# Zero-tile multiplications on TensorE during the first loads and maxima of an attention and two-layer kernel

## Chip, cores, metric

The kernel runs on one core of a Trainium2 chip. The metric is the device time of one execution in microseconds; lower is better. Engines are named as in the profile: PE is TensorE's matmul, PEld its weight load, DVE is VectorE, ACT ScalarE, POOL GpSimd, SP the engine that issues most DMAs.

## What is computed

Attention with queries that are averaged in pairs, then two feed-forward layers on its output (2304 tokens, width 512, inner width 2048):

```python
# q, k, v: (4, 8, 1152, 64)
q_pool = q.reshape(B, H, S // 2, 2, D).mean(axis=3)
scores = np.matmul(q_pool, k.transpose(0, 1, 3, 2)) / np.sqrt(D)
scores = scores - np.max(scores, axis=-1, keepdims=True)
attn = np.exp(scores)
attn = attn / (np.sum(attn, axis=-1, keepdims=True) + 1e-09)
x = np.matmul(attn, v)            # heads side by side: 2304 x 512
h = x @ moe_w_in
x = (h - np.tanh(h)) @ moe_w_out
r = np.maximum(x @ moe2_w_in, 0.0)
out = (s * (r * r) + b) @ moe2_w_out
```

## The kernel before

Attention goes by pairs of heads, 16 pairs. `prep(n)` prepares pair n: it adds neighbouring queries (L355), transposes queries (`ptq`, L361) and keys (`ptk`, L380) on TensorE, splits them into a rounded part and a rest (`U`, `T`, `ql`, `kl`), sends pieces to other partitions by DMA on SP's queue, and computes the maximum of every query's scores. For that it multiplies 128 queries by 384 keys into a PSUM tile `ptm` (L418 for pair 0, L420 for later pairs, L394 for the queries that are left over, `ptm_r`), and VectorE reduces each tile to one column (L421, L395). The loop runs over the two heads j, over groups s of 128 queries (four) and over key blocks i (three), so a head has twelve such steps. The maxima of a head are reduced once more (L423), transposed (`ptc`, L425) and moved to a row of `U2`, which the second part of each score multiplication (L460) takes in. `scores` computes transposed scores in two multiplications, L459 with 128 rows and L460 with 65, takes the exponential on ScalarE (L461), and `single` multiplies the result by the values (L532).

For pair 0 alone (L416 to L418) the maxima take one head's half of the partitions, so these multiplications have 64 rows; all others named here have 128 or 65 rows. PSUM tiles of `prep` come from a ring of four (`psP`).

While pair 0's maxima are computed, pair 1's queries and keys are loaded. All but the first two key loads are issued on SP's queue, in order. The tile framework keeps one order for each engine, and an engine takes its instructions strictly in that order. Pair 0's steps, pair 1's transposes and the first scores are interleaved in it by a clock of ticks; `tc.high_priority` moves an instruction ahead and `tc.issue_after` holds it behind another.

`rests` are two tiles of 128 x 128 that start as zeros; `prep(n)` writes the left-over queries of pair n into `rests[n % 2]` (L369).

Of the kernel before, what the change touches and what calls it, by code (L numbers as in the profile page):

```python
# [9 lines left out]
F32 = mybir.dt.float32  # L10
F32R = mybir.dt.float32r
# [7 lines left out]
P = 128  # L19
# [28 lines left out]
BATCH = 3  # L48
STORE, PUT = 8, 6
LINE, TOP = 32, 24  # L50

MOE_NS = 445
EVAC_NS = 250
# [2 lines left out]
SOON = 40  # L56
# [3 lines left out]
def f32(ap):  # L60
    return ap.bitcast(F32)
# [3 lines left out]
def attention_moe_moe_kernel(  # L65
# [19 lines left out]
    HB = SQ // 2  # L85
# [17 lines left out]
    mm = nc.tensor.matmul  # L103
    act = nc.scalar.activation
    dve = nc.vector
# [7 lines left out]
    pp = pctx.enter_context(tc.tile_pool(name="prep", bufs=1))  # L113
    fp = sctx.enter_context(tc.tile_pool(name="fin", bufs=1, side="right"))
    swp = sctx.enter_context(tc.tile_pool(name="sweep", bufs=1, side="right"))
    stage = actx.enter_context(tc.tile_pool(name="stage", bufs=1, side="right"))

    ident = cp.tile([P, P], F32, name="ident")
    make_identity(nc, ident)
# [35 lines left out]
    def line(pool, n, name, tag=None):  # L155
        return pool.tile([P, -(-n // LINE) * LINE], F32, tag=tag or name, name=name)[:, :n]

    def later(k, fn):
        queue.append((clock[0] + k, fn))
# [13 lines left out]
    class Weights:  # L173
# [63 lines left out]
        def put(self, which, f, i, cols, x):  # L237
            w = weight(f)
            if self.left > self.act_last:
                dve.tensor_copy(w[:, 2 * i, cols], x)  # L240
            else:
                act(w[:, 2 * i, cols], x, AF.Copy)
            added[0] = self.sub(w[:, 2 * i + 1, cols], x, f32(w[:, 2 * i, cols]))
# [61 lines left out]
    psV = actx.enter_context(tc.tile_pool(name="psV", bufs=1, space=PSUM))  # L305
# [17 lines left out]
    for j in range(2):  # L323
        dve.memset(f32(T2[j][D:D + 1, :]), 1.0)

    rests = [pp.tile([P, P], F32R, name=f"rest{i}") for i in range(2)]
    for rest in rests:
        dve.memset(f32(rest), 0.0)

    ops = {}  # L330

    def load_pair(n):
        b, hp = pairs[n]
        h0 = 2 * hp
        for j in range(2):
            dma(out=qrs[j], in_=q[b, h0 + j].rearrange("(t p r) d -> p t (r d)", p=QP, r=2))
        for j in range(2):
            put = nc.scalar.dma_start if n == 0 else dma
            put(out=kr[:, :, j, :], in_=k[b, h0 + j].rearrange("(p t) d -> p t d", t=NKT))
# [5 lines left out]
    def prep(n):  # L345

        T1, U1, ql = T1s[n % 3], U1s[n % 3], qls[n % 2]
        rest = rests[n % 2]
        kl = T1s[2][0] if n == 0 else kl1
        ops[n] = (T1, U1)  # L350

        for j in range(2):
            eng = dve if n == 0 else pool
            with tc.issue_after(added[0].ins) if n > 1 else ExitStack():
                eng.tensor_add(qrs[0][:, :, j * D:(j + 1) * D], qrs[j][:, :, 0:D], qrs[j][:, :, D:2 * D])  # L355
        yield 4 if n < 2 else 16
        for g in range(2):
            with tc.high_priority(offset=SOON):
                pt = psP.tile([P, KB], F32, tag="pp", name=f"ptq{n}_{g}")
                for i in range(3):  # L360
                    nc.tensor.transpose(  # L361
                        pt[:, i * QP:(i + 1) * QP],
                        qrs[0][:, 3 * g + i],
                        ident[:QP, :QP],
                    )
                act(U1[1][:, g * HB:(g + 1) * HB], pt[:, :HB], AF.Copy)
                h = slice((1 - g) * D, (2 - g) * D)
                q0 = g * (HB - MIX)
                act(rest[h, (1 - g) * MIX:(2 - g) * MIX], pt[h, q0:q0 + MIX], AF.Copy)  # L369
                dve.tensor_sub(  # L370
                    ql[:, g * HB:(g + 1) * HB], pt[:, :HB], f32(U1[1][:, g * HB:(g + 1) * HB])
                )
            yield 2
        for i in range(2):
            dma(out=f32(U1[0][i * D:(i + 1) * D, :]), in_=f32(U1[1][0:D, :]))
        for g in range(NKB):
            with tc.high_priority(offset=SOON):
                pt = psP.tile([P, KB], F32, tag="pp", name=f"ptk{n}_{g}")
                for i in range(3):
                    nc.tensor.transpose(  # L380
                        pt[:, i * P:(i + 1) * P],
                        kr[:, 3 * g + i].rearrange("p h d -> p (h d)"), ident)
                act(T1[1][:, g * KB:(g + 1) * KB], pt, AF.Copy)
                dve.tensor_sub(
                    kl[:, g * KB:(g + 1) * KB], pt, f32(T1[1][:, g * KB:(g + 1) * KB])
                )
            yield 2
        dma(out=f32(T1[0][0:D, :]), in_=f32(T1[1][0:D, :]))
        moved[0] = dma(out=f32(T1[0][D:P, :]), in_=f32(kl[0:D, :]))
        mps = [line(ap, (NQS + 1 - j) * NKB, f"mp{n}_{j}", f"mp{j}").rearrange("p (s i) -> p s i", i=NKB)  # L390
               for j in range(2)]
        for i in range(NKB):
            pt = psP.tile([P, KB], F32, tag="pp", name=f"ptm{n}_r_{i}")
            mm(pt, rest, T1[1][:, i * KB:(i + 1) * KB], start=True, stop=True)  # L394
            dve.reduce_max(mps[0][:, NQS, i:i + 1], pt, axis=AX.X)  # L395
            yield MAXSTEP
        def rest_moves():
            with tc.issue_after(moved[0].ins):
                dma(out=f32(U1[1][0:D, :]), in_=f32(U1[1][D:P, :]))
                dma(out=f32(T1[1][0:D, :]), in_=f32(kl[D:P, :]))  # L400

        if n > 0:
            rest_moves()
        if n + 1 < len(pairs):
            later(LOAD, lambda: load_pair(n + 1))
        yield GAP1 if n == 1 else GAP
        for j in range(2):
            ns = NQS + 1 - j
            mp = mps[j]
            m = line(ap, ns, f"m{n}_{j}", f"m{j}")  # L410
            for s in range(NQS):
                for i in range(NKB):
                    pt = psP.tile([P, KB], F32, tag="pp", name=f"ptm{n}_{j}_{s}_{i}")
                    kk = slice(i * KB, (i + 1) * KB)
                    q0 = s * P + j * MIX
                    if n == 0:  # L416
                        h = slice(j * D, (j + 1) * D)
                        mm(pt, U1[1][h, q0:q0 + P], T1[1][h, kk], start=True, stop=True)  # L418
                    else:
                        mm(pt, U1[j][:, q0:q0 + P], T1[j][:, kk], start=True, stop=True)  # L420
                    newest[0] = dve.reduce_max(mp[:, s, i:i + 1], pt, axis=AX.X)  # L421
                    yield MAXSTEP
            dve.reduce_max(m, mp, axis=AX.X)  # L423
            pt = psP.tile([P, KB], F32, tag="pp", name=f"ptc{n}_{j}")
            nc.tensor.transpose(pt[:ns, :P], m, ident)  # L425
            act(cs[j], pt[:ns, :P], AF.Copy, scale=-1.0)
            maxes.add((n, j))
            if n == 0 and j == 1:
                rest_moves()
            yield 1  # L430
# [235 lines left out]


    load_pair(0)
    moe = deque()
    preps = deque()  # L670
    pend = deque()

    def add_prep(n):
        preps.append([prep(n), clock[0]])
# [346 lines left out]
    for t in range(2):  # L1021
        for i in range(NBLK3):
            for p in range(t * RUN, (t + 1) * RUN):
# [13 lines left out]
                for x, (a, b) in enumerate(PRODUCTS):  # L1037
                    ps = Y if b in ("b21", "t1", "b22") else X
                    fresh_ = b in ("b11", "b21", "t1")
                    for h, (wa, xa) in enumerate(((0, 0), (0, 1), (1, 0))):  # L1040
                        for c in range(2):
                            mm(ps, u[a][:, (2 * wa + c) * P:(2 * wa + c + 1) * P], xs[b][xa][:, c],  # L1042
                               start=(fresh_ and h == 0 and c == 0), stop=(h == 2 and c == 1), skip_group_check=not fresh_)
# [73 lines left out]
```

## Time and profile before

| | us |
|---|---|
| median of 3 runs | 1342.68 |
| the three runs | 1341.97, 1342.68, 1345.07 |
| the profiled execution | 1345.31 |
| its span in the trace | 1343.5 |

| engine | busy us | share |
|---|---|---|
| PE | 1313.0 | 98% |
| PEld | 1128.4 | 84% |
| DVE | 947.9 | 71% |
| ACT | 634.2 | 47% |
| POOL | 346.9 | 26% |

The profiled execution took 1345.31 us, of which 1343.5 lie between the first and the last instruction. The busy time of PE runs from the issue of a matmul to the modelled end of its drain, so a share of 98% doesn't mean that it multiplies 98% of the time. The page's line of granted clock shows 0.7 of full speed in the first two of 40 slices (33.6 us each) and 0.9 or more, which the page writes as 9, in the others.

### The profile page before, as it was taken

The page shows a single profiled execution, that of the slowest core. Times are in us where ns is not written, and L with a number is a line of the kernel's source. Part 1 is how long each engine was busy: PE and PEld are TensorE (multiplying, and loading weights), DVE is VectorE, ACT ScalarE, POOL GpSimd, SP SyncE. Part 2 cuts the span into 40 slices and gives each one's busy share as a digit, 9 for nine tenths or more (in the row PEclk, how much of TensorE's full clock was granted, in tenths as well). Part 3 has the DMA queues.
Part 4 walks back from the last instruction along what each step waited for, and adds up shares of the span by engine and source line. Part 5 has one row for each costly group of instructions (what it writes and reads, how often), then busy time and mean ns, then how long its engine had stood idle before and what let it go on. Part 6 is the DMA issues. An engine that isn't in the chain of part 4 may idle for free.

```text
span 1343.5 us, 22384 instructions
## 1 busy us (share of the span) xinstructions
PE 1313.0 (98%) x8118; PEld 1128.4 (84%) x8118; DVE 947.9 (71%) x1888; ACT 634.2 (47%) x1527; POOL 346.9 (26%) x287
## 2 busy tenths in 40 slices
PE   6999999999999999999999999999999999999998
PEld 4677777777878778776999999999988889888887
DVE  6788895966665656659688577686878787656654
ACT  2355555555555555654333333333545454544532
POOL 0211157666777666774000000000000000000000
PEclk7799999999999999999999999999999999999999
DMA  8577766665657657444687124558334365404031
GB/s 176 138 172 174 177 143 155 151 168 133 163 118 175 143 124 173 97 112 144 199 280 229 54 82 132 153 169 265 118 118 139 120 204 165 157 0 141 1 94 48
DMA packets 203183, 191.61 MB, mean 143 GB/s; under 512 B 88640, under 2 KB 170688, under 8 KB 203072
## 3 DMA queue, kind: packets, MB, share of 16 engines
q1 hardware_dynamic: 200736, 189.59, 52.0%
q8 instruction: 64, 1.05, 0.3%
q10 hardware_dynamic: 2336, 0.59, 0.3%
q14 instruction: 47, 0.39, 0.1%
HBM read 115.34 MB, written 39.32 MB: 115 GB/s over the span
## 4 chain that ended last, share of the span: by engine, by line
PE 89%; DVE 6%; DMA 2%; ACT 1%; issue 1%; SPq 0%; POOL 0%; DVEq 0%; ACTq 0%; POOLq 0%
PE o L997 14%; PE h L823 11%; PE y L834 11%; PE pv L564 8%; PE h L1042 7%; PE s L459 6%; PE s L460 5%; PE k L1042 5%; PE ptm L420 5%; PE y L645 4%; PE h L632 3%; PE pv L532 2%; PE su L532 2%; PE ptk L380 1%; PE su L578 1%
## 5 line engine op out<-in xcount | busy, mean ns | idle before, releaser
L461 ACT ACTIVATE pf<-s 128x288 f32<-128x288 f32 x576 | 223.7, 409 | 168.4 <-PE s L460 163.2
L421 DVE TENSOR_REDUCE mp<-ptm 128x1 f32<-128x384 f32 x384 | 202.4, 544 | 110.7 <-PE ptm L420 101.9
L523 POOL TENSOR_TENSOR acc<-acc,pf 128x576 f32<-128x576 f32 x159 | 228.2, 1435 | 53.4 <-ACT pf L461 45.4
L459 PE MATMUL s<-U,T 128*128 128x288 f32 x576 | 193.8, 342 | 1.6 <-ACT pf L461 0.5
L460 PE MATMUL s<-U,T 65*128 65x288 f32 x576 | 174.3, 307 | 0.0
L834 PE MATMUL y<-ghb,w 128*128 128x288 f32 x784 | 172.1, 296 | 0.3 <-DVE yr L842 0.3
L823 PE MATMUL h<-xx,w 128*128 128x288 f32 x1176 | 170.3, 294 | 0.4 <-DVE thb L659 0.4
L823 PEld LDWEIGHTS h<-xx,w 128*128 128x128 f32 x1176 | 160.5, 188 | 0.6 <-DVE thb L659 0.6
L997 PE MATMUL o<-w,g2h 128*128 128x512 f32 x486 | 153.6, 392 | 0.0
L420 PE MATMUL ptm<-T,U 128*128 128x384 f32 x360 | 135.4, 383 | 2.7 <-DVE mp L421 1.9
L459 PEld LDWEIGHTS s<-U,T 128*128 128x128 f32 x576 | 110.9, 193 | 26.8 <-ACT pf L461 11.4
L834 PEld LDWEIGHTS y<-ghb,w 128*128 128x128 f32 x784 | 130.8, 188 | 0.6 <-DVE yr L842 0.6
L564 PE MATMUL pv<-pf,vo 128*64 128x288 f32 x864 | 120.7, 415 | 0.0
L460 PEld LDWEIGHTS s<-U,T 65*128 65x128 f32 x576 | 111.4, 194 | 7.3 <-issue 4.4
L834 PE MATMUL y<-glb,w 128*128 128x288 f32 x392 | 115.7, 295 | 0.0
L1042 PE MATMUL h<-w,w 128*128 128x384 f32 x522 | 106.8, 337 | 0.3 <-DVE w L908 0.2
L1042 PEld LDWEIGHTS h<-w,w 128*128 128x128 f32 x522 | 93.0, 188 | 9.8 <-DVE w L908 1.6
L997 PEld LDWEIGHTS o<-w,g2h 128*128 128x128 f32 x486 | 89.4, 188 | 10.0
L997 PE MATMUL o<-w,g2l 128*128 128x512 f32 x234 | 92.8, 397 | 0.0
L564 PEld LDWEIGHTS pv<-pf,vo 128*64 128x64 f32 x864 | 55.7, 136 | 41.1 <-issue 10.9
L958 ACT ACTIVATE r_c<-r_c 128x384 f32<-128x384 f32 x72 | 37.7, 524 | 109.2 <-DVE r_c L1054 52.8
L963 DVE SCALAR_TENSOR_TENSOR g2l<-r_c,spread,g2h 128x384 fp32r<-128x384 f32 x96 | 59.2, 616 | 39.5 <-ACT g2h L962 39.2
(145 smaller groups left out, 2377.6 us busy)
## 6 DMA issues: line engine op xcount, KB each, us to landing
xx<-x1d SPq DMA_DIRECT2D x80, 288.0 KB
T<-T SPq DMA_DIRECT2D x50, 288.0 KB
raw<-in_moe_w_in_dram SPq DMA_DIRECT2D x23, 512.0 KB
raw<-in_moe_w_out_dram SPq DMA_DIRECT2D x23, 512.0 KB
qr<-in_q_dram SPq DMA_DIRECT2D x32, 288.0 KB
vo<-in_v_dram SPq DMA_DIRECT2D x32, 288.0 KB
x1d<-xo SPq DMA_DIRECT2D x64, 144.0 KB
kr<-in_k_dram SPq DMA_DIRECT2D x30, 288.0 KB
```

The costliest lines, as they stand in the source:

```text
L420: mm(pt, U1[j][:, q0:q0 + P], T1[j][:, kk], start=True, stop=True)
L421: newest[0] = dve.reduce_max(mp[:, s, i:i + 1], pt, axis=AX.X)
L459: last[0] = mm(ps, T1[j][:, t * P:(t + 1) * P], U1[j][:, sl], start=True, stop=False)
L460: last[0] = mm(ps, T2[j][:, t * P:(t + 1) * P], U2[j][:, sl], start=False, stop=True)
L461: act(pf[:, sl], ps, AF.Exp, scale=SCALE)
L523: added[0] = pool.tensor_add(accs[n, j, r], old, pf)
L564: mm(po[g * D:(g + 1) * D], vos[j][:, u, 0:D], pf[:, g * HB:(g + 1) * HB], start=(t == 0 and i == 0), stop=(u == NKT - BATCH))
L823: mm(ps[:, :n], w[:, a, c * P:(c + 1) * P], xx[:, c, x, 0:n], start=(i == 0 and c == 0), stop=(i == 2 and c == NDC - 1))
L834: mm(ys[i][c], w[:, a, c * P:(c + 1) * P], x, start=(f == fa and r == 0), stop=(f == fb - 1 and r == 2))
L963: gates.append(dve.scalar_tensor_tensor(out=gl, in0=r, scalar=sb2[:, 1:2], in1=f32(gh), op0=ALU.add, op1=ALU.subtract))
L997: mm(os[r], g[:, k * P:(k + 1) * P], w[a], start=(first and n == half and x == 0), stop=(last and n != half and x == 2))
L1042: mm(ps, u[a][:, (2 * wa + c) * P:(2 * wa + c + 1) * P], xs[b][xa][:, c], start=(fresh_ and h == 0 and c == 0), stop=(h == 2 and c == 1), ...
```

## The change

The two `rest` tiles are made and cleared first of all, ahead of the other constants, in reverse order. A PSUM tile `idle` takes the buffer that pair 0's sums use later. A new function `spin(k)` issues k multiplications of `rests[1]` by itself, 128 rows by 128 columns, whose result nobody reads. It is called with 48 right after the first loads are issued; with 2 behind each maxima step of head 0 and behind the first three of head 1; and with 10 behind the first step of head 1's second group. The first transposes of pair 0 are held behind the 48.

```diff
+SPIN = 48, 2, 10
...
+    rests = [pp.tile([P, P], F32R, name=f"rest{i}") for i in range(2)]
+    for rest in reversed(rests):
+        dve.memset(f32(rest), 0.0)
+
     ident = cp.tile([P, P], F32, name="ident")
...
-    rests = [pp.tile([P, P], F32R, name=f"rest{i}") for i in range(2)]
-    for rest in rests:
-        dve.memset(f32(rest), 0.0)
+    idle = psV.tile([P, HB], F32, tag="su", name="idle")
+
+    spun = [None]
+
+    def spin(k, ins=None):
+        with tc.high_priority(offset=SOON), tc.issue_after(ins) if ins else ExitStack():
+            for _ in range(k):
+                spun[0] = mm(idle[:, :P], rests[1], rests[1], start=True, stop=True)
...
-            with tc.high_priority(offset=SOON):
+            with tc.high_priority(offset=SOON), tc.issue_after(spun[0].ins) if n == 0 else ExitStack():
                 pt = psP.tile([P, KB], F32, tag="pp", name=f"ptq{n}_{g}")
...
-                        mm(pt, U1[1][h, q0:q0 + P], T1[1][h, kk], start=True, stop=True)
+                        made = mm(pt, U1[1][h, q0:q0 + P], T1[1][h, kk], start=True, stop=True)
+                        if j == 0 or s == 0:
+                            spin(SPIN[1], made.ins)
+                        elif (s, i) == (1, 0):
+                            spin(SPIN[2], made.ins)
...
     load_pair(0)
+    spin(SPIN[0])
```

On TensorE, where pair 0's maxima begin, the order was this (the last number of a `ptm` name is only a serial number; before it stand head, group and key block):

```order
L394 MATMUL ptm_r_257<-T_0_1_170,rest_197 128x384 [waits DVE_49,Activation_49]
L418 MATMUL ptm_0_0_0_265<-T_0_1_170,U_0_1_176 128x384 [waits DVE_49]
L418 MATMUL ptm_0_0_1_268<-T_0_1_170,U_0_1_176 128x384 [waits DVE_49]
L418 MATMUL ptm_0_0_2_271<-T_0_1_170,U_0_1_176 128x384 [waits DVE_49]
L418 MATMUL ptm_0_1_0_274<-T_0_1_170,U_0_1_176 128x384 [waits DVE_49]
```

After the change it is this, at the same place on TensorE:

```order
L404 MATMUL ptm_r_306<-T_0_1_174,rest_75 128x384 [waits DVE_49,Activation_49]
L428 MATMUL ptm_0_0_0_314<-T_0_1_174,U_0_1_180 128x384 [waits DVE_49]
L338 MATMUL idle<-rest_76 128x128 x2
L428 MATMUL ptm_0_0_1_319<-T_0_1_174,U_0_1_180 128x384 [waits DVE_49]
L338 MATMUL idle<-rest_76 128x128 x2
L428 MATMUL ptm_0_0_2_324<-T_0_1_174,U_0_1_180 128x384 [waits DVE_49]
```

Two zero multiplications stand between any two of these steps, so twelve times in head 0 and three times in head 1 a multiplication of 64 rows is followed by two of 128 rows. The two first scores of L459, which stood ahead of head 0's last three steps, now stand behind them.

Where pair 1's keys come in, TensorE's order was this:

```order
L418 MATMUL ptm_1_1_0_358<-T_0_1_170,U_0_1_176 128x384 [waits DVE_49]
L361 MATMUL ptq_1_361<-ident,qr_181 128x96 [waits DVE_49]
L361 MATMUL ptq_1_361<-ident,qr_181 128x96 x2
L418 MATMUL ptm_1_1_1_373<-T_0_1_170,U_0_1_176 128x384 [waits DVE_49]
L380 MATMUL ptk_0_378<-ident,kr 128x128 [waits DMAHW1_49,DMAHW0_49,DVE_49]
```

After the change TensorE has there:

```order
L371 MATMUL ptq_1_450<-ident,qr_185 128x96 [waits DVE_49]
L371 MATMUL ptq_1_450<-ident,qr_185 128x96 x2
L428 MATMUL ptm_1_1_1_462<-T_0_1_174,U_0_1_180 128x384 [waits DVE_49]
L338 MATMUL idle<-rest_76 128x128 [waits Activation_49]
L338 MATMUL idle<-rest_76 128x128 x9
L390 MATMUL ptk_0_467<-ident,kr 128x128 [waits DMAHW1_49,DMAHW0_49,DVE_49]
```

The ten multiplications stand one step later than their call, between head 1's fifth step and the first transposes of pair 1's keys, and wait for ScalarE, which has by then written pair 1's left-over queries into `rests[1]`. Behind this place TensorE's order and that of SP, ScalarE and GpSimd are as before; VectorE's differs in its memsets and in two neighbouring swaps.

## Rows read from the trace of the kernel before

**Rows 1.** Busy time of each engine, granted clock (PEclk), DMA, by stretch.

```profile
core 0: us, PE busy (x) PEld busy (x) DVE busy (x) ACT busy (x) POOL busy (x), PEclk, DMA share, GB/s
...
7.90:11.64 3.74, 3.41 (x16) 2.93 (x17) 1.45 (x4) 2.02 (x7) 0.00 (x0) 1.00 0.54 161
11.64:15.06 3.42, 3.06 (x8) 1.27 (x7) 3.23 (x8) 0.49 (x1) 1.98 (x2) 1.00 0.84 192
15.06:26.90 11.84, 8.32 (x22) 4.81 (x21) 8.22 (x18) 1.41 (x5) 0.00 (x0) 0.50 1.11 213
26.90:49.20 22.30, 22.26 (x60) 14.49 (x61) 13.39 (x36) 6.91 (x17) 2.50 (x3) 0.50 0.47 121
```

**Rows 2.** Timeline of TensorE and VectorE, first twelve microseconds; idle time in brackets.

```profile
5.63 0.31 DVE L328 MEMSET rest<- 128x128 f32 x2
...
7.92 0.87 PE L361 MATMUL ptq<-ident,qr 96*128 96x96 f32 x4 [7.92 <-DVE qr L355]
...
10.70 0.90 PE L380 MATMUL ptk<-ident,kr 128*128 128x128 f32 x3 [0.31 <-DVE ql L370]
```

**Rows 3.** Timeline of TensorE, the maxima of pair 0 and the restart.

```profile
12.78 4.40 PE L418 MATMUL ptm<-T,U 64*128 64x384 f32 x9
...
17.88 1.32 PE L418 MATMUL ptm<-T,U 64*128 64x384 f32 x3
20.35 0.38 PE L425 MATMUL ptc<-ident,m 128*5 128x128 f32 x1 [1.15 <-DVE m L423]
20.66 1.32 PE L418 MATMUL ptm<-T,U 64*128 64x384 f32 x3
21.91 0.74 PE L361 MATMUL ptq<-ident,qr 96*128 96x96 f32 x3
...
23.87 0.69 PE L418 MATMUL ptm<-T,U 64*128 64x384 f32 x1
26.94 0.87 PE L380 MATMUL ptk<-ident,kr 128*128 128x128 f32 x3 [2.39 <-DMA kr<-in_k_dram]
```

**Rows 4.** Timeline of VectorE, the reductions of those maxima.

```profile
14.03 4.26 DVE L421 TENSOR_REDUCE mp<-ptm 128x1 f32<-128x384 f32 x9
18.60 1.49 DVE L421 TENSOR_REDUCE mp<-ptm 128x1 f32<-128x384 f32 x3 [0.31 <-PE ptm L418]
```

**Rows 5.** Chain of waits: start, length, what; in the half-clock stretch.

```profile
34.31 0.24 PE s L460
34.55 0.62 PE ptm L418
35.17 0.62 PE ptm_r L394
...
38.32 0.54 PE s L459
38.86 0.32 PE ptm_r L394
```

**Rows 6.** Timeline of the weight loads (PEld) in the half-clock stretch.

```profile
34.48 0.28 PEld L418 LDWEIGHTS ptm<-T,U 64*128 64x128 f32 x1 [0.28 <-issue]
35.09 0.29 PEld L394 LDWEIGHTS ptm_r<-T,rest 128*128 128x128 f32 x1 [0.33 <-DVE raw L228]
35.26 0.33 PEld L459 LDWEIGHTS s<-U,T 128*128 128x128 f32 x1
```

**Rows 7.** Chain of waits, the same multiplications at the full clock.

```profile
49.77 0.14 PE s L460
...
51.52 0.17 PE ptm L420
```

**Rows 8.** Timeline of TensorE, three transposes at the full clock.

```profile
68.88 0.49 PE L380 MATMUL ptk<-ident,kr 128*128 128x128 f32 x3
```

**Rows 9.** Stretches around 612 us, as in rows 1.

```profile
612.38:615.80 3.42, 1.80 (x12) 1.29 (x12) 3.35 (x6) 1.30 (x5) 2.30 (x3) 1.00 0.45 140
615.80:619.20 3.40, 3.40 (x15) 3.14 (x13) 3.40 (x10) 1.60 (x5) 0.73 (x1) 0.50 0.25 74
```

## Prediction

> **What bounds the kernel now.** I read the stretches first, then the chain of waits, then TensorE's timeline. Until 7.92 us TensorE waits for the queries and their addition [rows 2]. It then does transposes, and from 12.78 us the maxima of pair 0, which VectorE paces: nine reductions take 4.26 us and three 1.49, so one more costs (4.26 - 1.49) / 6 = 0.46 us [rows 4], and TensorE's nine steps take 4.40 us [rows 3]. Then TensorE idles 2.39 us for the load of pair 1's keys and restarts at 26.94 us [rows 3]. From there to 49.2 us TensorE is listed as busy for 22.26 of 22.30 us, VectorE for 13.39 [rows 1]: TensorE is the bound. A delay of the restart therefore reaches the end almost whole, and so does a gain.
>
> The granted clock is 1.2 GHz (0.50) from 15.06 to 49.2 us [rows 1]. That costs: 288 columns take 0.24 us there and 0.14 us at 2.4 GHz, 384 columns 0.32 and 0.17 [rows 5, 7]. Before 11.64 us the view prints 1.00, but three transposes at 10.70 us take 0.90 us, like those at 26.94 us under 0.50 (0.87) and unlike those at 68.88 us (0.49) [rows 2, 3, 8]; I take the engine to be at 1.2 GHz there too. So the kernel has a slow clock in its first 49 us, except for some 3 us.
>
> **The change, part by part.** *The 48.* One streams 128 columns. In the same number format 384 columns take 0.32 us at 1.2 GHz [rows 5], so 128 take 0.107 us and 48 take 5.1 us. VectorE clears `rests[1]` first of all; two such memsets take 0.31 us [rows 2], so they start near 1.1 us (estimate) and end near 6.2 us, under the wait that lasts until 7.92 us. This costs nothing. If one took as long as a transpose of 128 columns, 0.90 / 3 = 0.30 us [rows 2], they would end at 15.5 us and delay the start by 7.6 us; that is the upper bound, and I take the lower, since the format is that of the maxima. The gain is bounded by the transposes on the chain, some 2 us at 1.2 GHz (0.87 + 0.90 [rows 2] and a few between), of which a full clock would give back 1 us; below it is nothing.
>
> *The pairs of two.* They look free: 0.32 us and twice 0.107 make 0.53 us at 1.2 GHz, 0.17 and twice 0.06 make 0.29 at 2.4, against VectorE's 0.46. But each stands between two multiplications of 64 rows and has 128 rows itself. What such an alternation costs is in the trace at 34 us: the step of 64 rows occupies 0.62 us of the chain instead of 0.32, and so does the 128-row multiplication behind it (0.62; and 0.54 instead of 0.24 for scores), while the same `ptm_r` behind a 128-row multiplication takes 0.32 [rows 5]. The weight loads show why: that of the 64-row step has 0.28 us idle ahead of it and the one behind it 0.33, whereas the following one starts 0.17 us later, under the running multiplication [rows 6]. So each change of shape costs 0.30 us, and there are two in every step. A step then takes 0.32 + 0.214 + 0.60 = 1.13 us at 1.2 GHz, and TensorE takes VectorE's place as the pace.
>
> The Trainium skill, "TensorE: Matmul & The Clock Gate", section "Part 2: What happens when you issue a matmul", says that a weight load is pulled ahead of a running multiplication if the row groups don't conflict or if it goes to the background weight buffer. By its second case the alternation would be free and the step 0.53 us, so that 15 steps would cost 1 us and stay within the idle time; the idle times of the loads here say otherwise, and the measurement decides.
>
> *The sum, at 1.2 GHz throughout.* Head 0's twelve steps from 12.78 us: 12 x 1.13 = 13.6, so 26.3 us (before, 17.88 + 1.32 = 19.2 us [rows 3]). The last reduction, the small one and the transposed maxima: 1.0 us, as the 1.15 us ahead of `ptc` before [rows 3]; the two scores of L459 (2 x 0.24) lie under it. `ptc` to the next step 0.31 us (20.66 - 20.35): 27.6 us. Three steps of head 1: 3.4, so 31.0 us. From the queries' transposes to the end of head 1's fifth step as before, 23.87 + 0.69 - 21.91 = 2.65 us [rows 3]: 33.7 us. The ten: 0.30 + 10 x 0.107 = 1.4, so 35.0 us. The keys are there by 26.9 us as before, since SP's queue does not wait for these steps until the maxima's move. TensorE restarts at 35.0 instead of 26.94 us: 8.1 us later. Queued behind the ten are pair 1's key transposes and all scores, so everything waits.
>
> In this execution 2.4 GHz was granted from 11.64 to 15.06 us [rows 1]. If that comes again, a step there takes 0.17 + 0.12 + two changes. No row shows this change at 2.4 GHz; between 0.15 (halved) and 0.30 a step takes 0.59 to 0.89 us. I take 0.2 for a change, nearer the half because weights stream with the same clock: 0.69. The 2.3 us from 12.78 to 15.06 then hold 3.3 steps, each 0.44 cheaper: 1.5 us. The delay is 6.6 us, my value; bounds from both ends are 5 and 8.1.
>
> Work behind the restart is the same and, at 1.2 GHz, as long. The profiled execution at 1345.31 us would become 1351.9. It lies 2.6 us above the median of the runs, which I put down to how soon the clock comes back; I add the delay to the median: 1342.68 + 6.6 = **1349.3 us**.
>
> **Why the clock does not save it.** The multiplications aim at the granted clock, and whether it holds decides. What speaks against: from 26.9 to 45 us TensorE alternates between 64 and 128 rows as the new order does, is listed as busy all the time, and stays at 1.2 GHz [rows 1, 5]. After 612 us it idles for nearly half of a stretch, works in the rest, and gets 1.2 GHz behind it [rows 9]. And in the new order much of a step is an exposed weight load.
>
> **Rivals.** *A, the clock holds.* 2.4 GHz stays from the first transposes over the gap and through the bound stretch. Then steps take 0.69 us, 15 x 0.23 = 3.4 us more, which fit into the idle 1.15 + 2.39 us [rows 3]. The stretch of 22.3 us shrinks to VectorE's 13.39 [rows 1] and a waiting share of a tenth, 14.5 us: a gain of 7.8, up to 8.8 with the start. From the profiled execution that gives 1337.5, from the median 1335. For it speaks that streaming at half speed is the largest loss in these 49 us; against it the ten multiplications fill only 0.6 to 1.4 us of the gap before the keys. The Trainium skill, same page, section "Part 1: The HAM clock gate (the "warmup" mystery)", speaks for it: the throttled state is the default, and activity of TensorE releases it. Zeros are activity as well, if the rule counts them; no row here shows it.
>
> *B, the change does nothing that can be measured.* The clock stays as it was, and alternation is free or the idle time covers it (15 x 0.07 = 1 us at 0.53 a step): 1342.7 us. The point from which it decides is 0.23 us more for each of the 15 steps, 3.5 us in all. Against it stand the 0.60 us [rows 5].
>
> *C, worse.* The 48 run long by the upper bound and the delay adds up: 1342.7 + 6.6 and some 3 to 5 us more, 1353 to 1355.
>
> **How the numbers follow.** My forecast 0.60, A 0.20, B 0.15, C 0.05. A measurement tells about 0.2%, 2.7 us, from no change. Slower: 0.60 + 0.05 = 0.65, less 0.03 for runs whose clock returns early: 0.62. Faster: A, 0.20. Same: B and the 0.03, 0.18. The forecast's own range is 1345.5 to 1353 us (delay of 5 to 8.1 us, and 2.5 us either way for the return of the clock). The range of 8 in 10 takes in B and the near end of A: 1338 to 1354 us.
>
> **What would show it.** Right: steps of head 0 in TensorE's timeline 1.1 us apart once 0.50 is granted, VectorE's reductions waiting for `ptm`; `ptc` near 26 us; the first key transposes of pair 1 at 32 to 35 us, released by TensorE's own queue and not by the keys' load; 0.50 granted for most of 15 to 45 us. Wrong: steps 0.47 us apart, weight loads of the steps without idle time ahead of them, or 1.00 granted from 11 us on.

## The result, and the profile after

| | before | after |
|---|---|---|
| median of 9 runs each, us | 1341.63 | 1349.50 |
| single runs, us | 1336.64 to 1345.07 | 1347.27 to 1358.26 |
| the profiled execution, us | 1345.31 | 1358.26 |
| its span, us | 1343.5 | 1356.5 |
| first transposes of pair 0 | 7.92 | 11.35 |
| `ptc` of head 0 | 20.35 | 31.48 |
| restart: first key transposes of pair 1 | 26.94 | 40.08 |
| 2.4 GHz granted for good, behind the restart | 49.2 | 63.6 |

The ratio, which goes by all runs and not by the medians, is 1.0078 with a 95% interval of [1.0051, 1.0105]: slower by 0.8%, by 7.9 us in the medians and by 13.0 us between the two profiled executions. The predicted 1349.3 us lies 0.2 us beside the median. The traces say that this closeness is luck: the restart is late by 13.1 us and not by 6.6, and the median moved less than the restart did. The experiments are about both.

The stretches of the kernel after, to be held against [rows 1]; columns as there:

```profile
core 0: us, PE busy (x) PEld busy (x) DVE busy (x) ACT busy (x) POOL busy (x), PEclk, DMA share, GB/s
...
7.92:11.55 3.63, 3.63 (x20) 3.63 (x20) 0.00 (x0) 0.00 (x0) 0.00 (x0) 1.00 0.28 81
...
16.29:31.48 15.19, 15.19 (x40) 9.86 (x39) 8.01 (x16) 0.00 (x0) 1.99 (x2) 1.00 0.87 176
31.48:40.08 8.60, 8.60 (x29) 5.92 (x28) 3.15 (x6) 1.30 (x4) 0.00 (x0) 1.00 0.33 90
40.08:63.60 23.52, 23.52 (x66) 15.52 (x67) 13.83 (x37) 7.14 (x19) 2.61 (x3) 1.00 0.43 109
63.60:80.00 16.40, 16.40 (x87) 12.23 (x87) 14.31 (x33) 8.49 (x24) 4.27 (x5) 1.00 0.70 151
```

PEclk needs care here: this execution's first record of the clock stands at 63.60 us, and the view prints 1.00 ahead of it. The instructions tell otherwise: three transposes take 0.90 us at 14.12 and at 43.90 us, as under 0.50 before, and not 0.49 [rows 2, 8]. So the engine ran at 1.2 GHz until 63.6 us. Between 7.92 and 11.55 us TensorE is busy throughout while VectorE, ScalarE and GpSimd do nothing at all: they wait for the transposes, which stand behind the 48.

TensorE's timeline of the kernel after (start, length; idle time in brackets), beside [rows 2, 3]:

```profile
1.05 10.50 PE L338 MATMUL idle<-rest 128*128 128x128 f32 x48 [1.05 <-DVE rest L121]
11.35 0.86 PE L371 MATMUL ptq<-ident,qr 96*128 96x96 f32 x4
...
14.12 0.90 PE L390 MATMUL ptk<-ident,kr 128*128 128x128 f32 x3 [0.31 <-DVE ql L380]
...
16.22 0.69 PE L428 MATMUL ptm<-T,U 64*128 64x384 f32 x1
...
17.45 0.69 PE L428 MATMUL ptm<-T,U 64*128 64x384 f32 x1
18.07 0.69 PE L338 MATMUL idle<-rest 128*128 128x128 f32 x2
18.69 0.69 PE L428 MATMUL ptm<-T,U 64*128 64x384 f32 x1
...
31.48 0.41 PE L439 MATMUL ptc<-ident,m 128*5 128x128 f32 x1
...
37.89 2.39 PE L338 MATMUL idle<-rest 128*128 128x128 f32 x10
40.08 0.86 PE L390 MATMUL ptk<-ident,kr 128*128 128x128 f32 x3
...
43.90 0.90 PE L390 MATMUL ptk<-ident,kr 128*128 128x128 f32 x3
```

Three things are to be seen. The 48 last until 11.5 us, so one takes 0.213 us, twice the 0.107 us that the prediction took for its 128 columns. The steps of the maxima are 1.24 us apart (17.45 to 18.69), where nine took 4.40 us [rows 3]. And the restart at 40.08 us has no idle time ahead of it: TensorE's own queue releases it, and no wait for pair 1's keys is listed.

The weight loads (PEld) between the steps, and VectorE's reductions, in the kernel after:

```profile
18.07 0.50 PEld L338 LDWEIGHTS idle<-rest 128*128 128x128 f32 x2 [0.33 <-issue]
18.69 0.29 PEld L428 LDWEIGHTS ptm<-T,U 64*128 64x128 f32 x1
```

```profile
18.18 0.56 DVE L435 TENSOR_REDUCE mp<-ptm 128x1 f32<-128x384 f32 x1 [0.18 <-PE ptm L428]
19.41 0.56 DVE L435 TENSOR_REDUCE mp<-ptm 128x1 f32<-128x384 f32 x1 [0.68 <-PE ptm L428]
```

The idle 0.33 us ahead of the load behind a 64-row step is that of [rows 6]. VectorE, which set the pace before [rows 4], now waits 0.68 us in each step.

Two of the 48 and their weight loads, from the same kernel:

```profile
1.32 0.63 PE L338 MATMUL idle<-rest 128*128 128x128 f32 x2
1.43 0.55 PEld L338 LDWEIGHTS idle<-rest 128*128 128x128 f32 x2
```

A load starts 0.11 us behind the multiplication ahead of it, and the next multiplication 0.11 us behind its load: the two take turns, and together they make the 0.213 us.

The 13.1 us come apart by the marks of the table: 3.43 until the first transposes; nothing from there to the first step (4.86 us before, 4.87 after); 7.7 from the first step to `ptc` (7.57 before, 15.26 after); 2.0 from `ptc` to the restart (6.59 before, 2.39 of it idle; 8.60 after, none idle).

### The profile page after: what moved, and what is told of

It is laid out like the page before. It is cut to its first block, busy times and chain, and to the rows that moved or that the text cites. A ratio compares the mean times of both kernels' runs of the same rounds, so it can differ in the third digit from the quotient of the medians.

```text
span 1356.5 us, 22561 instructions
## 1 busy us (share of the span) xinstructions
PE 1336.0 (98%) x8206; PEld 1148.5 (85%) x8206; DVE 948.0 (70%) x1888; ACT 633.9 (47%) x1527; POOL 347.0 (26%) x287
## 4 chain that ended last, share of the span: by engine, by line
PE 90%; DVE 6%; DMA 1%; ACT 1%; issue 1%; POOL 0%; SPq 0%; DVEq 0%; ACTq 0%; POOLq 0%
PE o L1012 15%; PE y L849 11%; PE h L838 11%; PE pv L578 8%; PE h L1057 7%; PE s L473 6%; PE k L1057 6%; PE s L474 5%; PE ptm L434 5%; PE y L659 4%; PE h L646 3%; PE pv L546 2%; PE su L546 2%; PE idle L338 2%; PE ptk L390 1%; PE ptm L428 1%
## 5 line engine op out<-in xcount | busy, mean ns | idle before, releaser
L578 PEld LDWEIGHTS pv<-pf,vo 128*64 128x64 f32 x864 | 55.6, 136 | 41.1 <-issue 10.9
```

The source lines that it names most:

```text
L578: mm(po[g * D:(g + 1) * D], vos[j][:, u, 0:D], pf[:, g * HB:(g + 1) * HB], start=(t == 0 and i == 0), stop=(u == NKT - BATCH))
```

## The experiments

Each kernel was timed in five rounds beside the kernel before, except the last one. The kernel before gave medians of 1339.59, 1341.48 and 1344.18 us in the three sittings, each on another chip (31, 35 and 29 runs, single runs from 1335.38 to 1348.39). That spread is itself one of the questions, so ratios are within a sitting; they go by all runs, not by the medians.

### Each part alone

The 48 alone (without pairs and ten, the first transposes are held behind the 48 as in the change):

```diff
-SPIN = 48, 2, 10
+SPIN = 48, 0, 0
```

> The 48 alone; no pairs, no ten. Theory (each zero multiplication waits for its own weight load, 0.213 us at 1.2 GHz, twice what the streaming of 128 columns takes): the 48 end near 11.4 us, the first transposes start 3.4 us late (11.35 instead of 7.92 us), steps of the maxima stay 0.47 us apart, and the 2.39 us of idle time ahead of pair 1's keys take most of the delay: restart at 28.0 to 28.6 us instead of 26.94, time +1 to +2 us. Rival (the 0.213 us came from something else in the changed kernel, as the other added work): 0.107 us each, start at 7.9 us, restart at 26.9 us, time +0. Second rival (the 48 raise the clock): 1.00 granted behind them, transposes in 0.5 us, time -1 to -8 us.

Measured: 1349.88 us against 1339.59, ratio 1.0068 [1.0042, 1.0094]. The first transposes start at 11.35 us, as the theory said, but the restart is at 30.71 us and the idle time ahead of it has not shrunk. TensorE's timeline in this kernel, then SP's waits and SP's key loads (start and length of issue), the kernel before above this one:

```profile
30.71 0.87 PE L390 MATMUL ptk<-ident,kr 128*128 128x128 f32 x3 [2.73 <-DMA kr<-in_k_dram]
```

```profile
SPq L336 <- PE ptq L361: 1.1, 1, 1.1
SPq L346 <- PE ptq L371: 5.0, 1, 5.0
```

```profile
19.30 3.66 SPq L339 DMA_DIRECT2D kr<-in_k_dram  x2
22.72 3.01 SPq L349 DMA_DIRECT2D kr<-in_k_dram  x2
```

SP's queue stands 5.0 us instead of 1.1 at the load of pair 1's queries, because their buffer is released by pair 0's transposes. All that is queued behind it, pair 1's keys too, goes out late: at 22.72 us, where the kernel before issues them at 19.30. So the gap ahead of the keys moves along and takes up none of the delay. My expectation (28.0 to 28.6 us, +1 to +2 us) had missed this. Of the 10.3 us in the medians the restart explains 3.8. The traced execution took 6.3 us more than that of the kernel before, with the clock back equally late (22.8 and 22.3 us behind the restart); of these, 2.7 arise behind the attention. The other 4 us in the medians are open; a clock that comes late in more executions (all six lie from 1346.40 to 1351.58 us) would fit, and was not traced.

The pairs alone:

```diff
-SPIN = 48, 2, 10
+SPIN = 0, 2, 0
```

> The pairs alone; no 48, no ten. Theory (two changes of shape of 0.30 us in each step, and the zero multiplications at the pace of their weight loads): steps 1.24 us apart at 1.2 GHz, from 12.78 us as before; restart at 33.8 to 35.3 us instead of 26.94, time +7 to +8.4 us, less or more by up to 4 us by when the clock comes back. Rival (the pairs cost only what they stream and the late start of the changed kernel comes from the 48 and the ten): steps 0.53 us apart, restart at 27 to 28 us, time +1 us.

Measured: 1346.55 us against 1339.59, ratio 1.0054 [1.0026, 1.0081]; restart at 34.35 us, 7.4 us late, as the theory said. Its steps:

```profile
25.01 0.69 PE L428 MATMUL ptm<-T,U 64*128 64x384 f32 x1
25.63 0.69 PE L338 MATMUL idle<-rest 128*128 128x128 f32 x2
26.25 0.69 PE L428 MATMUL ptm<-T,U 64*128 64x384 f32 x1
```

The ten alone:

```diff
-SPIN = 48, 2, 10
+SPIN = 0, 0, 10
```

> The ten alone; no 48, no pairs. Theory: 0.30 + 10 x 0.213 = 2.4 us, which lies in the 2.39 us that TensorE idles before pair 1's keys: restart at 26.9 to 27.2 us, time within 0.5 us of before, clock not raised. Rival (they hold or raise the clock, since they fill the gap): 2.4 GHz soon behind the restart, the stretch that took 22.3 us takes 14.5, time -5 to -8 us.

Measured: 1340.72 us, ratio 1.0007 [0.9985, 1.0029]. They start in the gap and leave 0.75 us of it, and the clock is not back until 49.21 us:

```profile
24.04 1.52 PE L338 MATMUL idle<-rest 128*128 128x128 f32 x6
...
26.92 0.88 PE L390 MATMUL ptk<-ident,kr 128*128 128x128 f32 x3 [0.75 <-DMA kr<-in_k_dram]
```

The restarts add up: 3.8 for the 48, 7.4 for the pairs, and 2.2 for the ten (37.89 to 40.08), which are free alone and not in the changed kernel, where the gap is gone: 13.4 us, against 13.1 measured.

### Is it the change of shape?

The pairs alone again, but with zero operands of 64 rows, from the same half of the partitions as head 0's maxima. Nothing else differs from the run before; head 1's three pairs stay at 128 rows.

```diff
-    def spin(k, ins=None):
+    def spin(k, ins=None, h=slice(0, P)):
...
-                spun[0] = mm(idle[:, :P], rests[1], rests[1], start=True, stop=True)
+                spun[0] = mm(idle[:, :P], rests[1][h], rests[1][h], start=True, stop=True)
...
-                            spin(SPIN[1], made.ins)
+                            spin(SPIN[1], made.ins, h if j == 0 else slice(0, P))
```

> The pairs alone, but in head 0 the zero operands are 64 rows from the same half of the partitions as the maxima, so that the shape doesn't change (head 1's three pairs stay at 128 rows). Theory (the change of shape costs 0.30 us each, the weight load 0.213): steps of head 0 at 0.32 + 2 x 0.213 = 0.75 us at 1.2 GHz instead of 1.24; restart at 28.5 to 29.4 us, time +1.6 to +2.5 us (by the clock 4 us either way). Rival (shape does not matter; every weight load between other multiplications is exposed): steps stay at 1.2 us, restart at 34 to 35 us, time +7 to +8 us.

Measured: 1343.75 us, ratio 1.0021 [1.0000, 1.0043]; restart at 28.35 us. Two of its steps, and its waiting VectorE:

```profile
19.67 0.62 PE L428 MATMUL ptm<-T,U 64*128 64x384 f32 x1
20.10 0.52 PE L338 MATMUL idle<-rest 64*128 64x128 f32 x2
20.42 0.62 PE L428 MATMUL ptm<-T,U 64*128 64x384 f32 x1
```

```profile
15.11 0.56 DVE L435 TENSOR_REDUCE mp<-ptm 128x1 f32<-128x384 f32 x1 [0.19 <-PE ptm L428]
```

The step is 0.75 us instead of 1.24: same columns, same number of weight loads, only the rows differ. The two changes of shape cost 0.49 us a step. Between head 0's twelve steps lie eleven of these, 5.4 us; from the first step to `ptc` it takes 9.80 us instead of 15.25. The restart comes 6.0 us sooner, and the rest of that is an earlier start (first transposes at 7.26 instead of 7.79 us). This settles the mechanism. Without any pair the step is VectorE's 0.46 us, so the remaining 0.29 us is the price of the zero multiplications themselves.

### Ahead of the loads: what fits, and what raises the clock

28 in place of 48, nothing else:

```diff
-SPIN = 48, 2, 10
+SPIN = 28, 0, 0
```

> 28 instead of 48 zero multiplications ahead of the first transposes, no pairs, no ten: 28 x 0.213 = 6.0 us, which end near 7.1 us and so before the queries are there. Theory (the 48 alone cost what they do because they outlast the loads: 3.4 us late transposes, whose buffers SP's queue waits for before it can load pair 1): first transposes at 7.3 to 7.9 us, restart at 26.9 us, time within 2 us of before. Rival (zero multiplications ahead of the loads set when the clock comes back, and always late): start and restart as before, but time +4 to +6 us, since an execution in which the clock comes back some 22 us behind the restart takes 7.7 us longer than one in which it comes back after 7.5 us (1345.31 - 26.94 = 1318.4 against 1338.70 - 28.35 = 1310.4 in the runs so far).

Measured: 1341.72 us against 1341.48, ratio 1.000 [0.998, 1.002]; restart at 26.02 us. They end as the transposes can start:

```profile
1.05 6.23 PE L338 MATMUL idle<-rest 128*128 128x128 f32 x28 [1.05 <-DVE rest L121]
7.38 0.88 PE L371 MATMUL ptq<-ident,qr 96*128 96x96 f32 x4
```

So zero multiplications that end under the wait cost nothing here: what the 48 cost comes with the part that outlasts the loads. The restart is even 0.9 us earlier than before in this execution; why stays open.

24 of twice the width, from a zero tile of their own, nothing else:

```diff
-                spun[0] = mm(idle[:, :P], rests[1], rests[1], start=True, stop=True)
+                spun[0] = mm(idle[:, :256], zero[:, :P], zero, start=True, stop=True)
```

> 24 zero multiplications of 256 columns instead of 48 of 128, ahead of the first transposes alone; each streams as long as its weight load takes, 0.213 us at 1.2 GHz, so they end near 6.2 us, before the queries are there. Theory (the 48 left the clock at 1.2 GHz because they wait for their weight loads half of the time, not because they are zeros): 2.4 GHz is granted by 7.3 us, the first transposes take 0.5 instead of 0.9 us for three, SP's loads of pair 1 go out 1 to 2 us earlier, time -1 to -3 us. Rival (zeros do not raise the clock, however they stream): transposes at 0.9 us, time +0.

Measured: 1344.82 us against 1341.48, ratio 1.0013 [0.9991, 1.0035]. The clock does what the theory says, the time doesn't. Stretches and timeline of this kernel:

```profile
4.97:7.50 2.53, 1.00 (x8) 0.79 (x7) 2.13 (x3) 0.00 (x0) 0.00 (x0) 1.00 0.97 170
7.57:11.80 4.23, 3.22 (x19) 2.15 (x19) 2.49 (x6) 2.39 (x7) 0.00 (x0) 1.00 0.72 188
11.80:25.58 13.78, 10.42 (x27) 6.00 (x26) 10.29 (x23) 1.41 (x5) 1.98 (x2) 0.50 1.07 219
25.58:32.28 6.70, 6.70 (x23) 5.11 (x24) 4.27 (x13) 3.23 (x8) 0.00 (x0) 0.50 0.49 142
```

```profile
1.19 4.78 PE L341 MATMUL idle<-zero 128*128 128x256 f32 x24 [1.19 <-DVE zero L121]
...
9.82 0.55 PE L393 MATMUL ptk<-ident,kr 128*128 128x128 f32 x3 [0.91 <-DVE ql L383]
```

2.4 GHz is granted from 4.97 us, after 3.8 us of the wide ones; three transposes take 0.55 us; and the restart is 1.4 us earlier than before, but only 0.4 us earlier than behind the 28 narrow ones. But 1.2 GHz is back at 11.80 us, where VectorE paces the maxima and TensorE works only part of the time. The profiled execution took 1334.94 us, and 10 of the other 11 from 1341.80 to 1345.61. No trace of a longer one was taken, so why most of them give the gain back stays open.

### In the gap: width, number, and the 48 on top

Sixteen wide ones in place of the ten, nothing else (`zero` as above):

```diff
-SPIN = 48, 2, 10
+SPIN = 0, 0, 16
...
+                spun[0] = mm(idle[:, :256], zero[:, :P], zero, start=True, stop=True)
```

> 16 zero multiplications of 256 columns in place of the ten, no 48, no pairs: 0.30 + 16 x 0.213 = 3.7 us against 2.39 us of idle time, so the restart comes at 27.0 to 28.3 us instead of 26.94. Theory (continuous streaming brings the clock back in or right behind the gap): 2.4 GHz within 4 us of the restart in every execution, time -2 to -5 us and less spread than before. Rival (the clock does not count them): restart up to 1.3 us late, clock back 7.5 or 22 us behind it as in the other runs, time +0 to +1.5 us.

Ten wide ones:

```diff
-SPIN = 48, 2, 10
+SPIN = 0, 0, 10
...
+                spun[0] = mm(idle[:, :256], zero[:, :P], zero, start=True, stop=True)
```

> The ten alone, with 256 streamed columns instead of 128; nothing else of the change. Theory (each lasts as long as its weight load, 0.213 us at 1.2 GHz, and the clock is raised by streaming without pauses): they take no longer than the narrow ten and are hidden like these, restart at 26.9 us; the clock is back within 8 us of it in most executions: 1335 to 1339 us, perhaps not in all, since ten last only 2.1 us. Rival (the number or the length of the sixteen did it, not the width): as the narrow ten, 1340.7 us, spread of 10 us.

Sixteen of 128 columns, from `rests[1]` as in the change:

```diff
-SPIN = 48, 2, 10
+SPIN = 0, 0, 16
```

> Sixteen of 128 columns in the gap, nothing else: the same number, place and length in time as the sixteen wide ones that gave 1335.1 us, and half the columns. Theory (width decides): restart near 27.7 us, clock back 7 to 23 us behind it, 1340 to 1343 us with a spread of 10 us. Rival (filling the gap decides, by whatever): 1335 us, spread of 4 us.

| in the gap | median us | single runs | ratio to before |
|---|---|---|---|
| 16 of 256 columns | 1335.13 | 1332.57 to 1336.89 | 0.9950 [0.9932, 0.9969] |
| 10 of 256 | 1336.46 | 1334.20 to 1346.32 | 0.9965 [0.9941, 0.9989] |
| 16 of 128 | 1343.54 | 1339.16 to 1346.17 | 1.0007 [0.9987, 1.0027] |
| 10 of 128 (above) | 1340.72 | 1334.88 to 1345.49 | 1.0007 [0.9985, 1.0029] |

Each ratio is to the kernel before of the same sitting; 16 of 128 and 10 of 256 share one. The narrow ones multiply `rests[1]`, of which a quarter (64 x 64) holds left-over queries by then, and the wide ones multiply zeros alone. So the operands differ in more than width, and no run in the gap parts the two.

The timeline of the sixteen wide ones, then of the sixteen narrow ones, then the stretches of the former:

```profile
24.22 2.91 PE L341 MATMUL idle<-zero 128*128 128x256 f32 x12
...
27.67 0.73 PE L393 MATMUL ptk<-ident,kr 128*128 128x128 f32 x3
```

```profile
24.23 2.80 PE L338 MATMUL idle<-rest 128*128 128x128 f32 x12
...
27.57 0.90 PE L390 MATMUL ptk<-ident,kr 128*128 128x128 f32 x3
```

```profile
14.44:27.67 13.23, 12.09 (x38) 8.45 (x37) 7.93 (x18) 1.41 (x5) 0.41 (x1) 0.50 1.05 221
27.67:28.09 0.42, 0.42 (x3) 0.42 (x3) 0.31 (x1) 0.00 (x0) 0.00 (x0) 0.50 0.81 246
28.09:50.00 21.91, 21.91 (x109) 15.16 (x107) 19.71 (x55) 10.13 (x28) 4.55 (x6) 1.00 0.72 178
```

Wide and narrow ones hold TensorE equally long and delay the restart equally (27.67 and 27.57 us). The wide ones bring the clock back 0.42 us behind the restart in this execution, the narrow ones at 33.97 us, 6.4 us behind it, and of the 4.5 us between the two profiled executions 4.0 arise from there to pair 2's first key transposes. In time the wide ones gain and the narrow ones don't, at the same number and the same filling of the gap. The loads of the wide ones lie under the running multiplication:

```profile
25.00 0.63 PE L341 MATMUL idle<-zero 128*128 128x256 f32 x2
25.01 0.54 PEld L341 LDWEIGHTS idle<-zero 128*128 128x128 f32 x2
```

That wide ones bring the clock back at once in every execution is not shown: the run with wide ones in both places, below, is an exception. Of the ten wide ones, eight of twelve executions lie at 1339.13 us or below, but in the profiled one, of 1341.53 us, the clock came back only at 41.63.

Wide ones in both places:

```diff
-SPIN = 48, 2, 10
+SPIN = 24, 0, 16
...
+                spun[0] = mm(idle[:, :256], zero[:, :P], zero, start=True, stop=True)
```

> The 24 wide ones ahead of the loads and the 16 wide ones in the gap, no pairs. Theory: both gains, -3 to -8 us. Rival (no effect on the clock): +0 to +1.5 us.

Measured: 1335.02 us, ratio 0.9947 [0.9926, 0.9968]. Two gains were expected; the time is no better than that of the sixteen alone. Stretches from its restart at 27.33 us on:

```profile
27.33:35.28 7.95, 7.95 (x27) 5.97 (x26) 6.05 (x16) 3.92 (x10) 0.84 (x1) 0.50 0.40 92
35.28:50.00 14.72, 14.72 (x70) 10.15 (x70) 11.99 (x33) 4.58 (x13) 2.50 (x3) 1.00 0.65 174
```

Here sixteen wide ones stand in the gap, and the clock is back only 8.0 us behind the restart. This execution takes 1336.29 us all the same, because its work behind the attention is 3.3 us shorter than that of the sixteen alone, so a time near 1336 us doesn't tell by itself that the clock came back at once.

The 48 narrow ones of the change, and sixteen wide ones in the gap (w is 128 for the former and 256 for the latter):

```diff
-SPIN = 48, 2, 10
+SPIN = 48, 0, 16
...
+                spun[0] = mm(idle[:, :w], zero[:, :P], zero[:, :w], start=True, stop=True)
```

> The 48 narrow ones ahead of the loads as in the change, and sixteen wide ones in the gap; no pairs. Theory (what the 48 cost is 3.8 us of late restart and, beyond it, the late return of the clock): the wide ones take the second part away, restart at 30.7 to 32 us, and from there about 1309 us as in the other executions with an early clock: 1339 to 1341 us. Rival (the 48 cost 9 to 10 us by the loads, which stay late behind the restart): 1344 to 1346 us.

Measured: 1342.72 us, ratio 1.0009 [0.9990, 1.0029], between the two expectations. The clock is up at 30.70 us and the restart is at 31.32, 3.65 us behind that of the sixteen alone. From there the two traces run 3.5 us apart up to pair 15's transposes (546.8 and 550.3 us), so the loads don't stay late; the rest of their difference of 5.1 us arises behind the attention. The medians, from two sittings, differ by 7.6 us, of which the traces explain no more than these 5.1.

### The kernel before once more

Nothing is edited.

> The kernel before once more, for its clock. Theory (executions of one kernel differ by when the clock comes back behind the restart, at about 0.5 us of time for each us at half clock): restart at 26.9 us; time less restart is 1318 us if the clock is back 22 us behind it, 1315 after 16 us, 1310 after 7.5 us. Rival (they differ by something else, such as the loads): a time that does not fit these three pairs.

Measured: one execution, 1343.35 us. Its stretches:

```profile
11.11:14.52 3.41, 3.02 (x8) 1.24 (x7) 3.22 (x8) 0.44 (x1) 1.99 (x2) 1.00 0.83 188
14.52:26.95 12.43, 8.31 (x21) 4.85 (x22) 8.18 (x18) 1.41 (x5) 0.00 (x0) 0.50 1.04 199
26.95:41.83 14.88, 14.88 (x42) 10.03 (x42) 8.41 (x21) 5.28 (x13) 1.57 (x2) 0.50 0.54 149
41.83:60.00 18.17, 18.17 (x91) 13.06 (x91) 16.31 (x41) 8.71 (x24) 5.31 (x6) 1.00 0.80 176
```

The restart is where it was (26.95 us) and the clock is back 14.9 us behind it instead of 22.3. Time less restart is 1316.4 us, where the theory has 1315 for a return after 16 us: 1.4 us off, which lie in the last column of the table below (789.0 against 787.6 for the 28).

All traces together, in us from the start of each: the restart, how long behind it 2.4 GHz is granted for good, from the restart to pair 2's first key transposes, from there to pair 15's last key transposes, and the rest of the span.

| | restart | clock | to pair 2 | to pair 15 | rest |
|---|---|---|---|---|---|
| 48 narrow + 16 wide | 31.32 | -0.6 | 31.1 | 487.9 | 789.8 |
| 16 wide | 27.67 | 0.4 | 31.3 | 487.8 | 788.2 |
| 16 narrow | 27.57 | 6.4 | 35.3 | 489.2 | 787.4 |
| 24 wide ahead | 25.58 | 6.7 | 33.9 | 487.9 | 785.7 |
| pairs, 64 rows | 28.35 | 7.4 | 34.2 | 487.9 | 786.5 |
| pairs | 34.35 | 7.6 | 34.3 | 487.8 | 787.3 |
| 24 wide ahead + 16 wide | 27.33 | 8.0 | 34.4 | 487.8 | 784.9 |
| before, second | 26.95 | 14.9 | 37.5 | 488.1 | 789.0 |
| 10 wide | 26.51 | 15.1 | 37.6 | 487.8 | 787.9 |
| 28 ahead | 26.02 | 15.9 | 37.9 | 487.8 | 787.6 |
| before, first | 26.94 | 22.3 | 40.7 | 488.1 | 787.7 |
| 10 narrow | 26.92 | 22.3 | 40.8 | 487.8 | 788.2 |
| 48 | 30.71 | 22.8 | 41.1 | 487.6 | 790.4 |
| after | 40.08 | 23.5 | 41.4 | 487.7 | 787.3 |

The third column follows the second: 31 us with the clock at once, 41 with the clock 22 us late, 0.44 us for each us at 1.2 GHz. The fourth is the same within 0.5 us but for the 16 narrow ones. So a late restart reaches the end whole, and a late clock adds up to 10 us on top, whichever kernel it is. The rest scatters by 5.5 us, with no order that I can name. The clock also came back within 8 us of the restart in three kernels without the ten or the sixteen (24 wide ahead, and the pairs alone, of either kind), so an early return doesn't need them.

## Why the prediction held, and where it was wrong

**The 48** are the term that failed: "This costs nothing". One takes 0.213 us and not 0.107, so they end at 11.5 us; the delay of 3.43 us lies between the 0 that I took and the upper bound of 7.6. The step that failed is the overlap: the weight load was put under the running multiplication, and in the trace load and multiplication take turns, 0.11 us each. The Trainium skill, "TensorE: Matmul & The Clock Gate", section "LDWEIGHTS (loading the stationary operand)", gives a load's nanoseconds as its columns over 1.2, by an estimate 107 for 128 columns. The 0.11 us from a load's start to its multiplication agree with that. The second half of the mistake was "The keys are there by 26.9 us as before": SP's queue doesn't wait for the maxima, but it does wait for the transposes that the 48 hold back.

**The pairs** were right in mechanism, shown by the zero operands of 64 rows, and small in size: 1.24 us a step instead of 1.13. The two changes cost 0.49 us rather than 0.60, and the two zero multiplications, by the 64-row run, 0.43 rather than 0.214. The 1.5 us that a spell of 2.4 GHz was to give back did not come in this execution.

**The ten** took 2.2 us (37.89 to 40.08) instead of 1.4, by the same 0.213.

**The sum** to the restart was 6.6 us and measured 13.1. The excess of 6.5 comes out as 3.4 for the 48, 0.7 for the longer steps, 1.5 for the missing spell of clock, and 0.9 from `ptc` to the restart, for the ten above all.

**The median** nevertheless came out as forecast. "I add the delay to the median" took for granted that the clock comes back as it did before. By the table, an execution of the changed kernel takes 1358.3 us with the clock 23.5 us late and some 1348 to 1351 with the clock back within 8 us. Six of its nine lie from 1347.27 to 1350.04 us and three from 1354.28 to 1358.26, while those of the kernel before are spread from 1336.64 to 1345.07. That the clock came back sooner in most executions of the changed kernel is argued from these times; only one of them was traced, and the scatter behind the attention is of the same order. By this reading two errors, a delay too small and a fixed clock, cancelled: that the median lies 0.2 us beside the forecast is luck, and why the median rose less than the restart stays open.

**Rival A**, that the clock holds, was wrong for this change. Its number, 1335 us, is met by the sixteen wide ones at 1335.13, but not by its mechanism: there too 0.50 is granted from 14.44 to 28.09 us. The rule it drew on, that activity releases the throttle (the Trainium skill, same page, "Part 1: The HAM clock gate (the "warmup" mystery)"), agrees with the 24 wide ones (2.4 GHz after 3.8 us) and not with the 48 narrow ones (10.5 us in which TensorE is listed as busy, and still 1.2 GHz). **Rival B** fell with the step of 1.24 us. **Rival C** happened in its cause, the 48 that run long, and two of the runs (1356.82 and 1358.26) exceed even its 1353 to 1355 us.

**The signs** named ahead of time: steps 1.1 us apart (1.24), VectorE waiting for `ptm` (yes), `ptc` near 26 us (31.5, of it 3.4 for the 48), the restart at 32 to 35 us released by TensorE's own queue (40.1, so released), half clock for most of 15 to 45 us (throughout, by the instructions' lengths).

## What to carry to other kernels

Work that fills a wait must fit by its measured pace at the clock of that place, and the queues behind it must be followed too: here the loads of the next pair hung on the transposes behind the filler. Filler between multiplications of another row count pays for the change of shape twice; give it the same rows or leave it out. If filler is to raise the clock, try wide multiplications, which here cost no more than narrow ones, put them right ahead of the stretch that TensorE bounds, and read the granted clock there in more than one execution: here it was up at the restart in two of the three traces with sixteen of them.

## What the runs showed of the hardware that I had not expected

- Zero multiplications of 128 rows follow each other at 0.213 us at 1.2 GHz (48 in 10.5 us), and doubling their columns costs next to nothing: twelve of 256 columns last 2.91 us in the gap, twelve of 128 last 2.80. The weight load lies beside the running multiplication in the former and behind it in the latter; why isn't shown.
- Zeros can raise the clock: behind the 24 wide ones four transposes take 0.52 us in both traces, 0.87 before. The 48 narrow ones left them at 0.86 us in all three traces that have them.
- One kernel's executions differ by up to 13 us (1335.38 to 1348.39 for the kernel before, in one sitting). When 2.4 GHz returns behind the restart is part of it: 14.9 and 22.3 us in its two traces, which makes 3.2 us, and from at once to 23.5 us over all kernels, which makes 10. The Trainium skill, "TensorE: Matmul & The Clock Gate", section "Part 1: The HAM clock gate (the "warmup" mystery)", says that the chip's look at the engine's activity runs freely and doesn't begin with the kernel, so that the moment of a change varies from run to run, by some 0.5 us either way. Here too it varies, but by 7.4 us between two executions of one kernel, and no run shows that cause.
- The printed clock is 1.00 ahead of an execution's first record, whatever the engine does; the lengths of like instructions tell.
